# Mamba2 SSD and a low-rank mixer on one core: the sum of two operand parts is made on GpSimd in two operations instead of on VectorE in one

## The chip, the cores and the metric

The kernel runs on one core of one Trainium2 chip. The metric is the device time of one execution in microseconds (us); lower is better. The kernel before takes 227.7 us, the median of three runs (227.44 to 227.95).

A core has five engines that matter here: TensorE (PE; its weight loads are shown apart as PEld), VectorE (DVE), ScalarE (ACT), GpSimd (POOL) and the queue that issues transfers (SP). Each works off its own instructions in the order in which they were issued and waits on semaphores for the others.

## The reference

Two blocks follow each other. The first is a chunked state-space scan over 4 batches, 8 heads, 768 positions, head size 32 and state size 16. Its output, put back into (batch, position, 256 channels), is `x` of the second block:

```
def _moe_ref(x, U, V, w_ch1, w_ch2):
    xt = x.transpose(0, 2, 1)
    h = xt @ U @ V
    u = x + h.transpose(0, 2, 1)
    ch = np.maximum(u @ w_ch1, 0.0) @ w_ch2
    return (u + ch).astype(np.float32)
```

`w_ch1` is 256x1024 and `w_ch2` is 1024x256. The second block's weights arrive as 64-bit floats, which the kernel reads as pairs of 32-bit words and turns into float32; all else is float32.

## The kernel before

**Scan.** The scan goes over pairs of 128-position blocks. Its words in the plans are one-letter steps (`P`, `D`, `T`, `g`, `s`, `m`, `M`, `u`, `i`, `n`, `j`, `y`, `t`), each a short function that issues matmuls, VectorE masks and ScalarE copies.

**Mixer.** `mixer(b)` handles a batch in two halves (`j`) of 384 positions. `x` and `a` add the low-rank product to the scan's output; the result `u` lies as [128 channels, 2, 384]. Batch 0 multiplies in plain float32 (`plain`, word `U`). Batches 1 to 3 split each float32 factor into parts of a rounded format (`FP32R`) and sum three products:

- `near` is the factor times 1-2^-13, rounded; ScalarE makes it.
- `far` is the factor minus `near`; VectorE makes it.
- `both` is `far - near/4096` (`EPS` is 2^-12); `joined` makes it.

The weights have the matching three parts `w1[0..2]` and `w2[0..2]`, made once by `refine`. With `terms` the first two products (near with near, low with far) go into one PSUM bank, ScalarE scales the bank by 1+2^-12 (`scaled`), and the third product (the weights' `both` with the data's `both`) is added to it. So the third part is the last operand that TensorE reads in every sum.

**The steps.**

- `split(j)` (word `S`): near on ScalarE (L769), then `halves`: far on VectorE and `joined`, all three of 128x768, into one tile `u` that has one buffer. Batches 1 to 3 have two each, six in all.
- `first(j, m)` (word `f`): four matmuls into a bank `x` or `z`, two with near and two with far of `u`; then `scaled` (L779).
- `second(j, m)` (word `e`): two matmuls with `both` of `u`; then ScalarE makes near of the hidden activation (L808), with the ReLU.
- `third(j, m)` (word `h`): VectorE makes far of the activation from the bank and near (128x384). After every second `m`, a pair of 128x768 is whole, and `joined` makes its third part. Four pairs per half, 24 in all.
- `down(j)` or, for the second half of batch 3, `rows(j)` (word `d`): the products with `w2`, near first, far next, `both` last.

The parts of the hidden activation lie in a ring of 15 buffers called `words`, which the weights' words, two outputs and temporaries also use. Three buffers go to each pair.

**What sets the order.** The schedule is manual: `PLANS` lists the steps as words, and `follow` issues them one by one, so each engine's order is that of the words. Line 170 is the helper through which every VectorE operation passes, so all VectorE rows carry it; line 774 is `products`, through which the mixer's matmuls pass. GpSimd builds masks at the start (L294, L308, L309) and does four products and three slot products of the scan's first batch (L479, L591); the last of them starts at 20.84 us. All transfers are issued on SP.

A stretch of the plan of batch 4 (the last), with a split and what follows it:

```
'x1 h2.1.6 h2.1.7 d2.0 d2.1 a1.0 a1.1 d2.1 S1.0 d2.1 d2.1 d2.1 f1.0.0 d2.1 d2.1 f1.0.1 '
'd2.1 d2.1 e1.0.0 h1.0.0 e1.0.1 d2.1 d2.1 h1.0.1 f1.0.2 f1.0.3 d2.1 e1.0.2 f1.0.4 e1.0.3 '
...
'h1.0.6 h1.0.7 d1.0 d1.0 d1.0 d1.0 S1.1 d1.0 d1.0 f1.1.0 d1.0 f1.1.1 e1.1.0 d1.0 d1.0 '
```

Of the kernel before, what the change touches and what calls it, by code (L numbers as in the profile page):

```python
# [10 lines left out]
FP32 = mybir.dt.float32  # L11
# [10 lines left out]
EPS = 2.0 ** -12  # L22
AF = mybir.ActivationFunctionType
ALU = mybir.AluOpType
# [52 lines left out]
def kernel(  # L77
# [27 lines left out]
    nc = tc.nc  # L105
# [53 lines left out]
    class Kept:  # L159
# [15 lines left out]
    vector = Kept(nc.vector)  # L175
# [7 lines left out]
        out=a_sb,  # L183
# [128 lines left out]
    for v in range(2):  # L312
        half = slice(v * H, v * H + H)
        vector.tensor_tensor(out=ref[half, half], in0=upto[half, half],
                                in1=low[v][half, half], op=ALU.subtract)
# [13 lines left out]
    for g in range(2):  # L329
# [3 lines left out]
        out=la.rearrange("p b c h -> p b h c"),  # L333
        in0=la_ps.rearrange("p g (b h c) -> p (g b) h c", h=NH, c=NC),
        scalar1=1e-6, scalar2=1.0, op0=ALU.max, op1=ALU.min)
# [17 lines left out]
    for v in range(2):  # L353
        half = slice(v * H, v * H + H)
        vector.tensor_scalar(out=causal[half], in0=upto[half, half], scalar1=-1.0,
                                scalar2=None, op0=ALU.mult)
# [359 lines left out]
    def mixer(b):  # L716
# [37 lines left out]
        def halves(near, far, both, v):  # L754

            vector.tensor_tensor(out=far, in0=v, in1=near.bitcast(FP32), op=ALU.subtract)
            joined(near, far, both)

        def joined(near, far, both):

            vector.scalar_tensor_tensor(out=both, in0=near.bitcast(FP32), scalar=-EPS,
                                           in1=far.bitcast(FP32), op0=ALU.mult, op1=ALU.add)

        def split(j):

# [44 lines left out]
        def third(j, m):  # L810

            near, far, both = gs[j, m // 2]
            vector.scalar_tensor_tensor(
                out=far[:, m % 2], in0=gs["t", j, m], scalar=0.0,
                in1=near[:, m % 2].bitcast(FP32), op0=ALU.max, op1=ALU.subtract)
            if m % 2:
                joined(near, far, both)
# [210 lines left out]
```

## Time and profile before

| | |
|---|---|
| median of three runs | 227.7 us (227.44 to 227.95) |
| span of the profiled execution | 225.2 us |
| instructions | 6994 |
| granted TensorE clock | 1.00 |
| ScalarE waiting for TensorE's `x` bank, L779 | 27.6 us, 20 times |
| VectorE waiting for ScalarE's near, L808 | 16.6 us, 18 times |
| VectorE far of a pair's half, 128x384 | 48 operations, 0.55 us each |
| VectorE far of a split, 128x768 | 6 operations, 0.95 us each |
| transfers | 14.56 MB, 31.9% of the transfer engines' time |

The profile shows one execution. The span goes from the first to the last instruction; the 2.5 us between it and the median lie around the program. A row of a group names the line, the engine, the operation, the tiles (written <- read), the shape and the count; then busy time and the mean duration in ns, and after the second bar the time for which the engine stood idle before them, with what ended it. A row in order of time begins with start and duration in us. A row of waits gives the total in us, how often, and the longest.

### The profile page before, as it was taken

To read this page: it belongs to the slowest core of one execution; us is meant where nothing else is said; L and a number is where in the kernel's file an instruction comes from. 1 tells how busy PE (TensorE), PEld (TensorE's weight loads), DVE (VectorE), ACT (ScalarE), POOL (GpSimd) and SP (SyncE) were. 2 spreads that over 40 slices of the span, in tenths; PEclk is the share of its full clock that TensorE was granted. 3 is DMA by queue.
4 is the path that set the end of the run, shared out by engine and by line. 5 is a ranking of instruction groups with operands and counts; after the bars stand their busy time and mean duration, and the time that the engine had idled before them with its cause. 6 is when DMAs were issued, how large, how long until landed. Compare 5 with 4: busy or idle time off the path is not lost.

```text
span 225.2 us, 6994 instructions
## 1 busy us (share of the span) xinstructions
PE 217.0 (96%) x3016; PEld 180.5 (80%) x3016; DVE 157.3 (70%) x339; ACT 120.8 (54%) x283; POOL 6.2 (3%) x22
## 2 busy tenths in 40 slices
PE   7978899999999999999999999999999999999994
PEld 5657676665666678768999998799998799999993
DVE  3388899897996767879538827978557925765641
ACT  2353765579875425754616615385356434934820
POOL 4022000000000000000000000000000000000000
PEclk9999999999999999999999999999999999999999
DMA  6889779981950023642006200200000100010022
GB/s 89 141 120 147 113 171 220 240 177 41 167 76 4 0 73 41 89 59 73 4 3 90 75 1 3 76 0 0 4 0 3 43 30 0 3 68 3 0 70 70
DMA packets 69294, 14.56 MB, mean 65 GB/s; under 512 B 63568, under 2 KB 67472, under 8 KB 69264
## 3 DMA queue, kind: packets, MB, share of 16 engines
q1 hardware_dynamic: 69264, 14.13, 31.9%
q8 instruction: 23, 0.38, 0.7%
q14 instruction: 7, 0.06, 0.1%
HBM read 10.98 MB, written 3.15 MB: 63 GB/s over the span
## 4 chain that ended last, share of the span: by engine, by line
PE 89%; SPq 5%; DVE 2%; DMA 2%; issue 1%
PE x L774 33%; PE z L774 31%; SPq L196 4%; PE y L678 4%; PE y L654 4%; PE w L728 3%; PE w L901 2%; PE w L699 2%; PE x L528 2%; DMA bc<-in_C_dram 2%; PE w L496 2%; PE w L563 2%; PE x L739 2%; PE z L528 1%; PE z L739 1%
## 5 line engine op out<-in xcount | busy, mean ns | idle before, releaser
L170 DVE SCALAR_TENSOR_TENSOR words<-words 128x768 fp32r<-128x768 f32 (+6 forms) x44 | 34.6, 804 | 2.1 <-ACT words L420 1.1
L774 PE MATMUL z<-u,w 128*128 128x384 f32 x144 | 33.0, 349 | 0.0
L774 PE MATMUL x<-u,w 128*128 128x384 f32 x144 | 32.7, 346 | 0.0
L779 ACT ACTIVATE x<-x 128x384 f32<-128x384 f32 (+1 forms) x31 | 14.6, 470 | 28.2 <-PE x L774 27.6
L774 PEld LDWEIGHTS z<-u,w 128*128 128x128 f32 x144 | 25.0, 188 | 1.4 <-ACT z L779 0.2
L774 PEld LDWEIGHTS x<-u,w 128*128 128x128 f32 x144 | 24.9, 188 | 1.0
L774 PE MATMUL x<-words,w 128*128 128x384 f32 x120 | 24.7, 340 | 0.2 <-DVE yT L170 0.2
L774 PE MATMUL z<-words,w 128*128 128x384 f32 x120 | 24.6, 336 | 0.0
L779 ACT ACTIVATE z<-z 128x384 f32<-128x384 f32 (+1 forms) x30 | 14.2, 473 | 14.7 <-PE z L774 14.1
L170 DVE SCALAR_TENSOR_TENSOR words<-x,words 128x384 fp32r<-128x384 f32 x24 | 13.3, 553 | 11.7 <-ACT words L808 11.7
L774 PEld LDWEIGHTS x<-words,w 128*128 128x128 f32 x120 | 20.8, 188 | 0.5 <-DVE yT L170 0.4
L774 PEld LDWEIGHTS z<-words,w 128*128 128x128 f32 x120 | 21.1, 188 | 0.0
L170 DVE TENSOR_TENSOR yT<-x,yT 128x384 f32<-128x384 f32 x15 | 8.3, 553 | 16.0 <-PE x L774 15.4
L170 DVE SCALAR_TENSOR_TENSOR words<-z,words 128x384 fp32r<-128x384 f32 x24 | 13.2, 551 | 5.0 <-ACT words L808 5.0
L808 ACT ACTIVATE words<-x 128x384 fp32r<-128x384 f32 x24 | 11.8, 492 | 6.5 <-PE x L774 6.5
L808 ACT ACTIVATE words<-z 128x384 fp32r<-128x384 f32 x24 | 11.8, 492 | 4.5 <-PE z L774 4.5
L170 DVE TENSOR_TENSOR yT<-z,yT 128x384 f32<-128x384 f32 x15 | 8.3, 552 | 8.3 <-PE z L774 8.3
L654 PEld LDWEIGHTS y<-T,Sm 32*64 32x64 f32 x352 | 8.6, 131 | 4.7 <-issue 1.4
L654 PE MATMUL y<-T,Sm 32*64 32x64 f32 x352 | 11.9, 238 | 0.5 <-DVE settled L170 0.5
L678 PEld LDWEIGHTS y<-M,x 64*32 64x32 f32 x768 | 8.7, 105 | 4.5 <-issue 2.7
L678 PE MATMUL y<-M,x 64*32 64x64 f32 x768 | 11.3, 224 | 1.0 <-issue 0.7
L170 DVE SCALAR_TENSOR_TENSOR S<-S,kept,w 128x64 f32<-128x64 f32 x40 | 11.2, 279 | 1.6
(139 smaller groups left out, 382.3 us busy)
## 6 DMA issues: line engine op xcount, KB each, us to landing
words<-in_moe_w_ch_dram SPq DMA_DIRECT2D x7, 512.0 KB, 5.4
x<-in_x_dram SPq DMA_DIRECT2D x24, 128.0 KB, 3.5
out_dram<-o SPq DMA_DIRECT2D x5, 384.0 KB, 2.5
bc<-in_B_dram SPq DMA_DIRECT2D x24, 64.0 KB, 3.5
bc<-in_C_dram SPq DMA_DIRECT2D x12, 128.0 KB, 3.1
out_dram<-words SPq DMA_DIRECT2D x2, 384.0 KB, 3.6
words<-in_moe_w_ch_dram SPq DMA_DIRECT2D x2, 256.0 KB, 3.7
out_dram<-o SPq DMA_DIRECT2D x3, 128.0 KB, 1.7
```

Of the source, the lines that this page charges most:

```text
L170: self.last = call(*args, **kwargs)
L196: op = nc.sync.dma_start(**kwargs)
L496: nc.tensor.transpose(out=tp[:, i, v], in_=s["BC"][:, i, c + v].rearrange("p h n -> p (h n)"), identity=ident)
L528: nc.tensor.matmul(out=g[r][cols, c], lhsT=s["T"][rows, 0, c, cols], rhs=s["Cm"][rows, :, :, ts(2 * c + p, Q)].rearrange("r v t i -> r v i ...
L563: nc.tensor.matmul(out=s["A"][p][ts(r, Q), v], lhsT=s["bd"][half, v, 2 * r:2 * r + 2].rearrange("p h n -> p (h n)"), rhs=x_sb[k][half, v, ...
L654: product = nc.tensor.matmul(out=y[p][ts(r % 2, H), r // 2, c], lhsT=own[ts(r, Q)], rhs=s["T"][ts(r, Q), 1, :, ts(2 * c + p, Q)].rearrange ...
L678: product = nc.tensor.matmul(out=y[p][ts(i, Q), n, c], lhsT=x_sb[k][half, c, h], rhs=s["M"][half, h // 2, c, h % 2], start=fresh(k, p, [i] ...
L728: nc.tensor.matmul(out=p[ts(q, Q)], lhsT=U_sb[:, c], rhs=ytok[b][:, c, ts(q // 2, P)], start=(c == 0), stop=(c == NC - 1), skip_group_chec ...
L739: nc.tensor.matmul(out=h[q][:, :HS], lhsT=pT[rows], rhs=V4[rows], start=True, stop=True, skip_group_check=True)
L774: nc.tensor.matmul(out=t, lhsT=lhsT, rhs=rhs, start=start, stop=True, skip_group_check=True)
L779: nc.scalar.activation(t, t, AF.Copy, scale=1.0 + EPS)
L808: nc.scalar.activation(gs[j, m // 2][0][:, m % 2], t, AF.Relu, scale=NEAR)
```

## The change

`joined` no longer makes the third part in one VectorE operation. GpSimd first writes near times -2^-12 into the third part, and then adds far to it, in place. The value is the same, because the scaling by a power of two is exact. Both callers, `halves` (the splits) and `third` (the pairs), are affected; the weights' own third parts in `refine` stay on VectorE. No other line changes.

```diff
 def joined(near, far, both):
-    vector.scalar_tensor_tensor(out=both, in0=near.bitcast(FP32), scalar=-EPS,
-                                   in1=far.bitcast(FP32), op0=ALU.mult, op1=ALU.add)
+    nc.gpsimd.tensor_scalar(out=both, in0=near.bitcast(FP32), scalar1=-EPS, scalar2=None,
+                            op0=ALU.mult)
+    nc.gpsimd.tensor_tensor(out=both, in0=both.bitcast(FP32), in1=far.bitcast(FP32),
+                            op=ALU.add)
```

In the built programs VectorE has 30 operations fewer and GpSimd 60 more, in 30 pairs, after its last one of the prologue. The scaling waits for ScalarE (near) and for the buffer to be free; the addition waits for VectorE (far) and for the scaling. The order on TensorE, ScalarE and SP is the same. The scaling's line in the changed kernel is L761, the addition's L763.

## The prediction

> **What bounds the kernel now.** I read the busy shares first, then the chain that ended last, then a table of stages, and then TensorE's weight loads with their waits, since a busy matmul row alone proves little.
>
> ```profile
> PE 217.0 (96%) x3016; PEld 180.5 (80%) x3016; DVE 157.3 (70%) x339; ACT 120.8 (54%) x283; POOL 6.2 (3%) x22
> PE 89%; SPq 5%; DVE 2%; DMA 2%; issue 1%
> core 0: us, PE busy (x) PEld busy (x) DVE busy (x) ACT busy (x) POOL busy (x), PEclk, DMA share, GB/s
> 178.00:217.00 39.00, 38.86 (x240) 38.62 (x241) 23.36 (x36) 20.96 (x46) 0.00 (x0) 1.00 0.09 31
> ```
>
> The chain is TensorE for 89% and VectorE for 2%. In the stage from 178 to 217 us weight loads fill 38.62 of 39.00 us, at a granted clock of 1.00: there is nothing to win there. VectorE is busy for 60% of it. The changed line runs only after 80.8 us, and from 78 us on TensorE's weight loads wait for VectorE in six groups: 0.6, 0.4, 0.3, 0.2, 0.2 and 0.2 us, 1.9 us together. Three of them:
>
> ```profile
> PEld y L654 <- DVE settled L170: 0.6, 2, 0.4
> PEld x L774 <- DVE yT L170: 0.4, 1, 0.4
> PEld y L654 <- DVE S L170: 0.2, 1, 0.2
> ```
>
> **The change, part by part.** *Removed:* 30 VectorE operations (24 on `words`, 6 on `u`) of 0.958 us, 28.7 of its 157.3 us busy.
>
> ```profile
> L170 DVE SCALAR_TENSOR_TENSOR words<-words 128x768 fp32r<-128x768 f32 x24 | 23.0, 958 | 0.8
> L479 POOL TENSOR_TENSOR bd<-bc,FD 128x256 f32<-128x256 f32 x2 | 1.2, 620 | 7.4 <-ACT FD L385 7.4
> L479 POOL TENSOR_TENSOR bd<-bc,FD 128x128 f32<-128x128 f32 x2 | 0.8, 407 | 1.2 <-DMA bc<-in_B_dram 1.2
> L294 POOL TENSOR_SCALAR_AFFINE_SELECT low<-ones 128x128 f32<-128x128 f32 x2 | 0.5, 294 | 0.0
> L294 POOL TENSOR_SCALAR_AFFINE_SELECT after<-after 128x64 f32<-128x64 f32 x1 | 0.2, 240 | 0.1
> ```
>
> What this saves on the path is bounded above by the 1.9 us of waits. Most of it isn't there to be had: before the `yT` wait VectorE itself was idle, and the `settled` ones are a hand-over from TensorE and back. Only the 0.2 us for `S` (at 106.8 us) follows a removed operation. I take a gain of 0.1, between 0 and 0.2.
>
> *Added:* 60 GpSimd operations of 128x768. No row has them. The additions grow by (620-407)/128 = 1.66 ns an element, so 0.62+512x1.66 = 1.47 us; I use 1.45. The scaling has one input, like the selects: (294-240)/64 = 0.84 ns an element, 0.294+640x0.84 = 0.83 us. With 0.07 us between two dependent GpSimd operations (the gap in the prologue's selects) one sum takes 2.35 us, 30 take 70 us, half of the 137 us from 80 to 217. From below, DVE's 0.96 us for one pass bounds each; from above I allow twice my price (4.7 us a sum), as the formats with rounded output never ran on GpSimd here.
>
> The Trainium skill speaks against the change. "GPSIMD Engine Reference", § 3.1 Elementwise, gives a two-input addition of 2048 elements 4497 ns on GpSimd; at that rate 768 take 1.69 us, an estimate, and site F below would lose 0.7 us more over its three additions.
>
> *Moved:* the scaling waits for near alone, which ScalarE ends about 1 us before VectorE has made far, so on a free GpSimd it hides beside far, and the sum comes 1.45-0.96 = 0.5 us later than before. GpSimd's queue holds nothing else after 20.84 us: no DMA is issued there, none is passed. Behind a waiting addition stands the next scaling, nothing more. ScalarE's and VectorE's writes into the rings now wait for GpSimd's reads of the same buffer, but that buffer is some five pairs old; I cost this at nothing, hidden by that distance.
>
> *Who needs the sum, and when.* It is the last operand of its product. For the 24 pairs the products with near and with far come first, 32 matmuls that start 0.12 to 0.17 us apart, a cover of about 4 us; the last pair, far done at 215.2, gets its sum at about 217.1, and the products that use it start near 218.0. For the six splits the first readers are the two matmuls of `second`. Far's end plus 1.5 us against that reader: 83.3 against 86.2 (A); 106.0 against 106.2 (B); 147.1 against 147.3 (C); 161.5 against 163.2 (D, behind a pair); 182.0 against 185.7 (E). The sixth (F) comes behind two pairs:
>
> ```profile
> 195.94 0.96 DVE L170 SCALAR_TENSOR_TENSOR words<-words 128x768 fp32r<-128x768 f32 x1
> 197.86 0.96 DVE L170 SCALAR_TENSOR_TENSOR words<-words 128x768 fp32r<-128x768 f32 x1
> 198.74 0.95 DVE L170 TENSOR_TENSOR u<-yT,u 128x768 fp32r<-128x768 f32 x1
> 199.72 0.96 DVE L170 SCALAR_TENSOR_TENSOR u<-u 128x768 fp32r<-128x768 f32 x1
> 201.86 0.51 PE L774 MATMUL x<-u,w 128*128 128x384 f32 x2
> ```
>
> Far of the first pair is ready at 195.90, so GpSimd runs addition, scaling, addition, scaling, addition from 196.2: 3x1.45+2x0.83+4x0.07 = 6.3, to 202.5. The matmul wanted it at 201.8: TensorE stalls 0.7 us, and being full it never makes that up.
>
> *The unknown: both engines reading SBUF at once.* At a split, GpSimd's scaling and VectorE's far wait for the same near. Far has two SBUF operands. At C there is no room:
>
> ```profile
> 143.65 0.84 ACT L769 ACTIVATE u<-yT 128x768 fp32r<-128x768 f32 x1 [0.95 <-DVE yT L170]
> 144.62 0.95 DVE L170 TENSOR_TENSOR u<-yT,u 128x768 fp32r<-128x768 f32 x1
> 145.62 0.30 PEld L774 LDWEIGHTS x<-u,w 128*128 128x128 f32 x2
> ```
>
> Near ends at 144.49, far at 145.57, and the weight load that goes with far's first product starts 0.05 us later. If far had to wait out a scaling begun at 144.49, it would end 0.7 us later, and so would TensorE. The lower bound is no hindrance. The nearest rows:
>
> ```profile
> 10.70 1.20 POOL L479 TENSOR_TENSOR bd<-bc,FD 128x256 f32<-128x256 f32 x2 [7.37 <-ACT FD L385]
> 11.78 0.41 DVE L170 TENSOR_TENSOR BC<-bc,F 128x256 f32<-128x256 f32 x1
> ```
>
> They overlap for 0.12 us, and VectorE's 0.41 us are its usual ones. That is too short to tell. The upper bound is waiting in full: A 0.15, B 0.4 (far behind the scaling, 0.33, the rest behind `bd`), C 0.7, D 0.3 (0 to 0.55, by who goes first), E 0, and F 1.3 in place of 0.7 (1.0 if the far of the split waits for a pair's addition, 1.6 if it goes before a scaling); 2.85 in all.
>
> "SBUF — State Buffer", § Who interferes with whom, says that a VectorE instruction with two SBUF inputs and a GpSimd one that reads SBUF lock each other out in full. By that rule the sum is its upper bound, +2.75; without it, +0.6.
>
> **The sum.** No hindrance: 0.7-0.1 = +0.6. Full waiting: 2.85-0.1 = +2.75. The overlap row can't choose, so I take the middle, +1.7. The profiled execution spans 225.2 us, the runs' median is 227.7: 2.5 us around the span that nothing here touches. 225.2+1.7+2.5 = **229.4 us**.
>
> **The rivals.**
>
> *Latency alone* (+0.6, 228.3 us): only F stalls. For it: the overlap row shows no lengthening. Against it: that overlap is 0.12 us.
>
> *GpSimd becomes the bound.* At 4.7 us a sum the 30 need 141 us from 80.8 on, to 221.8; from the first product of the last sum to the end are 7.2 us (218.0 to 225.2): 229.0+2.5 = 231.5. In the last stage, where ten sums come in the 34.7 us from 180.5 to 215.2, stalls that can't be made up would bring it near 235. It decides from 3.5 us a sum. For it: unseen operations. Against: rows that make 2.35.
>
> *VectorE was the hidden limit* (faster). In front of the 0.2 to 0.6 us waits stands VectorE's in-order queue with 0.96 us sums in it; freed of them it brings S, M, yT and ytok earlier. At most 1.9 us: 225.8. It decides if a waiting TensorE had a removed sum directly ahead on VectorE, and GpSimd's reads cost VectorE under 0.2 us. Against: weight loads at 99% in the last stage, VectorE idle before `yT`.
>
> *It does nothing* (227.7): the sums hide, F included, if GpSimd's additions take under 1.2 us.
>
> **Chances.** A measurement here tells about 0.2% (0.46 us) from no change. Latency with waiting in part or full 0.55, latency alone 0.22 (0.12 of it within 0.2%), GpSimd as bound 0.12, relief 0.08, nothing 0.03. So faster 0.08, same 0.15, slower 0.77. The range leaves out half of the GpSimd bound and most of relief: its low end is just under no change (227.5), its top lies above full waiting (227.7+2.75 = 230.5) and one us into the bound's 231.5 to 235, at 232.5.
>
> **What would show it.** Right: GpSimd rows at L761 and L763 of 0.8 and 1.45 us, 60 of them, some 70 us; VectorE at 129 us unless lengthened; a new TensorE wait for GpSimd at F of 0.7 us or more; far of the splits late by up to 0.8 us, C the clearest. Wrong: a scaling far above 0.83 us, a sum late in the pairs' products, or VectorE's one-SBUF-input rows (0.55 us) longer beside GpSimd, which would delay everything and isn't in my sum. Unmoved rows and no new wait mean that nothing happened.

## The result, and the profile after

The changed kernel takes 259.92 us (median of four runs, 258.03 to 260.15) against 227.82 us (227.44 to 228.01) for the kernel before, measured together: a ratio of 1.138, 95% interval 1.135 to 1.142, or 32.1 us more. The forecast was 229.4 us with a range up to 232.5. Its direction held; its size was off by a factor of about 19 (+1.7 expected, +32.1 found).

The profiled execution spans 257.9 us, 32.7 more than before. First its page: busy time by engine, the granted clock in 40 slices, the chain that ended last, and the new groups.

```profile
PE 228.9 (89%) x3016; PEld 189.9 (74%) x3016; DVE 133.3 (52%) x309; ACT 121.7 (47%) x283; POOL 127.5 (49%) x82
...
PEclk9999999999999999979999997997799999959989
...
PE 59%; POOL 21%; issue 7%; SPq 5%; DVE 4%; ACT 2%; DMA 1%; POOLq 1%; ACTq 0%; DVEq 0%
...
L761 POOL TENSOR_SCALAR words<-words 128x768 fp32r<-128x768 f32 x24 | 51.3, 2137 | 30.8 <-ACT words L810 29.6
L763 POOL TENSOR_TENSOR words<-words 128x768 fp32r<-128x768 f32 x24 | 44.2, 1843 | 2.0
L761 POOL TENSOR_SCALAR u<-u 128x768 fp32r<-128x768 f32 x6 | 15.0, 2495 | 72.6 <-ACT u L771 72.2
```

The scaling takes 2.14 us where 0.83 was forecast, the addition 1.84 where 1.45 was. With two gaps of about 0.08 us a sum holds GpSimd for 4.1 us, not 2.35. GpSimd stands for 21% of the chain, TensorE for 59% instead of 89%. GpSimd's mean share of 49% hides that it has no free time in long stretches, of which the longest are 89.4 to 110.7, 157.7 to 178.2, 187.5 to 204.1 and 210.65 to 227.1 us.

Next TensorE's weight loads after 78 us, by what they waited for (total us, times, longest):

```profile
PEld x L776 <- POOL u L763: 15.2, 5, 7.0
PEld x L776 <- POOL words L763: 5.9, 3, 3.4
PEld x L776 <- DVE u L170: 1.6, 1, 1.6
```

That is 22.7 us of new waits. The span splits another way without remainder: TensorE was busy for 217.0 us before and idle for 225.2-217.0 = 8.2; after it was busy for 228.9 and idle for 29.0. So 20.8 us are idle time and 11.9 us are the same 3016 matmuls taking longer. The granted clock accounts for most of the latter: its mean is 0.954, not 1.00, and TensorE's busy time multiplied by the missing share of the clock, summed over windows of one microsecond, gives 10.6 us.

The longest stall shows both. GpSimd in order of time, ahead of the last split (site F of the prediction):

```profile
210.65 2.13 POOL L761 TENSOR_SCALAR words<-words 128x768 fp32r<-128x768 f32 x1 [0.81 <-ACT words L810]
212.87 1.85 POOL L763 TENSOR_TENSOR words<-words 128x768 fp32r<-128x768 f32 x1
214.80 2.14 POOL L761 TENSOR_SCALAR words<-words 128x768 fp32r<-128x768 f32 x1
217.02 1.85 POOL L763 TENSOR_TENSOR words<-words 128x768 fp32r<-128x768 f32 x1
218.96 2.13 POOL L761 TENSOR_SCALAR words<-words 128x768 fp32r<-128x768 f32 x1
221.17 1.80 POOL L763 TENSOR_TENSOR words<-words 128x768 fp32r<-128x768 f32 x1
223.05 2.13 POOL L761 TENSOR_SCALAR u<-u 128x768 fp32r<-128x768 f32 x1
225.27 1.80 POOL L763 TENSOR_TENSOR u<-u 128x768 fp32r<-128x768 f32 x1
```

And ScalarE's near for the last of these pairs and for the split, then TensorE, all of the same execution:

```profile
214.31 0.52 ACT L810 ACTIVATE words<-z 128x384 fp32r<-128x384 f32 x1
214.70 0.87 ACT L771 ACTIVATE u<-yT 128x768 fp32r<-128x768 f32 x1
...
219.54 0.86 PE L776 MATMUL z<-u,w 128*128 128x384 f32 x4
227.12 1.01 PE L776 MATMUL x<-u,w 128*128 128x384 f32 x2 [6.72 <-POOL u L763]
227.93 1.48 PE L776 MATMUL z<-words,w 128*128 128x384 f32 x4
```

The split's near is there at 215.57, but its scaling starts at 223.05: 7.5 us behind the pairs in GpSimd's queue. TensorE has done what stands ahead of the split's sum by 220.4 and stands still. The four matmuls before the stall take 0.86 us, the four after it 1.48 us. The same place in windows of one microsecond (length; busy us and count of PE, PEld, DVE, ACT and POOL; granted clock; transfers):

```profile
224.00:225.00 1.00, 0.00 (x0) 0.00 (x0) 0.00 (x0) 0.00 (x0) 1.00 (x1) 1.00 0.00 0
225.00:226.00 1.00, 0.00 (x0) 0.00 (x0) 0.00 (x0) 0.00 (x0) 0.92 (x2) 0.61 0.00 0
226.00:227.00 1.00, 0.00 (x0) 0.00 (x0) 0.00 (x0) 0.00 (x0) 1.00 (x1) 0.50 0.00 0
...
231.00:232.00 1.00, 1.00 (x5) 1.00 (x4) 0.00 (x0) 0.49 (x1) 0.06 (x1) 0.50 0.00 0
232.00:233.00 1.00, 1.00 (x7) 1.00 (x7) 0.55 (x2) 0.00 (x0) 1.00 (x1) 0.97 0.00 0
```

Here the clock falls to half about 5 us after the last matmul and is back about 5 us after the next one. That is not its rule: at C a standstill of 1.87 us was enough, and the clock fell at about 157.0, when TensorE was already at work again (two rows of TensorE, then a window):

```profile
153.36 0.85 PE L776 MATMUL x<-u,w 128*128 128x384 f32 x4
156.08 0.62 PE L776 MATMUL x<-u,w 128*128 128x384 f32 x2 [1.86 <-POOL u L763]
...
156.00:160.00 4.00, 3.92 (x14) 3.93 (x15) 1.20 (x3) 2.27 (x6) 2.25 (x3) 0.62 0.00 0
```

In windows of 0.2 us this execution has five stretches at half clock: three of 3.4 us and two of 6.8 us. "TensorE: Matmul & The Clock Gate", Part 1, in the Trainium skill states a half rate after an idle window of about 3.4 us and full rate after a busy one as long. The trace agrees on the two rates (0.50 and 1.00) and, by the length of the low stretches, on the window; that a shorter standstill can be enough is what it shows beyond this.

Last, the two engines at SBUF, at the split B:

```profile
104.19 1.83 POOL L763 TENSOR_TENSOR words<-words 128x768 fp32r<-128x768 f32 x1
104.33 2.51 DVE L170 TENSOR_TENSOR u<-yT,u 128x768 fp32r<-128x768 f32 x1
```

VectorE's far takes 2.51 us instead of 0.95: it begins 0.14 us after GpSimd's addition and ends 0.82 us after it. At C it is the other way about: far (from 151.20) and the scaling (from 151.18) start within 0.02 us of each other, far keeps its 0.95 us, and the scaling takes 2.96 us instead of 2.13.

### The profile page after: what moved, and what is told of

It reads as the page before. It is cut to its first block, busy times and chain, and to the rows that moved or that the text cites. A ratio compares the mean times of both kernels' runs of the same rounds, so it can differ in the third digit from the quotient of the medians.

```text
span 257.9 us, 7092 instructions
## 1 busy us (share of the span) xinstructions
PE 228.9 (89%) x3016; PEld 189.9 (74%) x3016; DVE 133.3 (52%) x309; ACT 121.7 (47%) x283; POOL 127.5 (49%) x82
## 4 chain that ended last, share of the span: by engine, by line
PE 59%; POOL 21%; issue 7%; SPq 5%; DVE 4%; ACT 2%; DMA 1%; POOLq 1%; ACTq 0%; DVEq 0%
PE x L776 22%; PE z L776 21%; POOL words L761 8%; POOL words L763 6%; SPq L196 4%; POOL u L763 4%; POOL u L761 3%; PE y L678 3%; PE y L654 3%; PE w L728 2%; DVE words L170 2%; PE x L528 1%; PE w L699 1%; DMA bc<-in_B_dram 1%; PE w L496 1%
## 5 line engine op out<-in xcount | busy, mean ns | idle before, releaser
L761 POOL TENSOR_SCALAR words<-words 128x768 fp32r<-128x768 f32 x24 | 51.3, 2137 | 30.8 <-ACT words L810 29.6
L761 POOL TENSOR_SCALAR u<-u 128x768 fp32r<-128x768 f32 x6 | 15.0, 2495 | 72.6 <-ACT u L771 72.2
L776 PE MATMUL x<-u,w 128*128 128x384 f32 x144 | 36.3, 372 | 14.9 <-POOL u L763 13.6
L763 POOL TENSOR_TENSOR words<-words 128x768 fp32r<-128x768 f32 x24 | 44.2, 1843 | 2.0
L776 PEld LDWEIGHTS x<-u,w 128*128 128x128 f32 x144 | 27.2, 206 | 17.6 <-POOL u L763 15.2
L776 PE MATMUL z<-u,w 128*128 128x384 f32 x144 | 34.9, 365 | 0.0
L776 PE MATMUL x<-words,w 128*128 128x384 f32 x120 | 26.9, 358 | 2.0 <-POOL words L763 1.8
L776 PEld LDWEIGHTS z<-u,w 128*128 128x128 f32 x144 | 26.8, 200 | 1.4 <-ACT z L781 0.2
L776 PE MATMUL z<-words,w 128*128 128x384 f32 x120 | 26.8, 358 | 0.0
L776 PEld LDWEIGHTS z<-words,w 128*128 128x128 f32 x120 | 23.0, 203 | 0.0
L654 PE MATMUL y<-T,Sm 32*64 32x64 f32 x352 | 11.9, 238 | 0.6 <-DVE settled L170 0.6
```

The costliest lines, as they stand in the source:

```text
L654: product = nc.tensor.matmul(out=y[p][ts(r % 2, H), r // 2, c], lhsT=own[ts(r, Q)], rhs=s["T"][ts(r, Q), 1, :, ts(2 * c + p, Q)].rearrange ...
L761: nc.gpsimd.tensor_scalar(out=both, in0=near.bitcast(FP32), scalar1=-EPS, scalar2=None, op0=ALU.mult)
L763: nc.gpsimd.tensor_tensor(out=both, in0=both.bitcast(FP32), in1=far.bitcast(FP32), op=ALU.add)
L776: nc.tensor.matmul(out=t, lhsT=lhsT, rhs=rhs, start=start, stop=True, skip_group_check=True)
```

## The experiments

Two theories had to be told apart. The first, the queue (Q where a letter is used): a sum costs GpSimd 4.1 us by itself, so sums pile up. The second, the ports (P): GpSimd's reads and VectorE's two-operand operations keep each other waiting, so both are slow and everything behind them too. All ratios are against the kernel before in the same series.

### Only the six splits, and only the 24 pairs

```diff
-        def joined(near, far, both):
+        def joined(near, far, both, pool=True):
+            if pool:
                 nc.gpsimd.tensor_scalar(...)
                 nc.gpsimd.tensor_tensor(...)
+            else:
+                vector.scalar_tensor_tensor(...)
...
             if m % 2:
-                joined(near, far, both)
+                joined(near, far, both, False)
```

This is the first, with the calls shortened. The second passes `False` in `halves` and leaves the pairs' call as it was.

> The six sums of the splits are made on GpSimd as in the change, the 24 sums of the pairs on VectorE as before. Theory Q (queue: a sum takes GpSimd 2.13+1.84 us, and TensorE waits for sums that stand in GpSimd's queue behind others): without pairs ahead of them the splits wait only for their own 4 us. Site A, D and E hide it, B loses about 1.7, C about 2.2, F about 0.4: 4.3 us, so 232 us (230 to 234), granted clock above 0.98. Theory P (port: GpSimd's reads of SBUF lengthen VectorE's work, and that costs the time): a fifth of the GpSimd work, a fifth of the 32 us, 234 us.

> The 24 sums of the pairs are made on GpSimd, the six of the splits on VectorE. Theory Q: the last pair's sum ends near 221 where 218.0 is wanted, 3 us, with a lower clock after it 1.5 more, and one or two us at the other halves: 234 us (231 to 238). With the splits alone this comes to far less than the 32 us of both, as the long stalls (7.0, 3.1 us) arise where a split stands behind three pairs. Theory P: four fifths of the GpSimd work, four fifths of the loss, above 250 us.

The splits alone take 231.47 us against 227.28 (ratio 1.019, 1.013 to 1.024), inside the range of the queue theory and 2.5 us under the 234 of the ports. The pairs alone take 242.62 us (1.066, 1.060 to 1.072), between the two expectations: a miss for both. The rows of TensorE's waits for GpSimd, the splits alone first:

```profile
PEld x L780 <- POOL u L764: 2.9, 2, 2.2
```

```profile
PEld x L780 <- POOL words L764: 9.0, 5, 3.8
```

The parts add up to 4.2+15.3 = 19.5 us, while both together cost 32. The other 12.6 us appear only when both share one queue: then a split waits behind its pairs, as at F. Part of this difference is the clock after the longer stalls: busy time multiplied by the missing clock is 3.4 us in the profiled execution of the pairs alone and nothing in that of the splits alone, against 10.6 us with both. (These two executions were the fastest of their kernels, so the difference at the medians is smaller.)

### VectorE makes every sum, GpSimd does the same work into memory that nothing reads

```diff
+    spare = const.tile([P, 2, 384], FP32, name="spare")
...
+            vector.scalar_tensor_tensor(out=both, in0=near.bitcast(FP32), scalar=-EPS,
+                                           in1=far.bitcast(FP32), op0=ALU.mult, op1=ALU.add)
-            nc.gpsimd.tensor_scalar(out=both, in0=near.bitcast(FP32), scalar1=-EPS, scalar2=None,
+            nc.gpsimd.tensor_scalar(out=spare, in0=near.bitcast(FP32), scalar1=-EPS, scalar2=None,
                                     op0=ALU.mult)
-            nc.gpsimd.tensor_tensor(out=both, in0=both.bitcast(FP32), in1=far.bitcast(FP32),
+            nc.gpsimd.tensor_tensor(out=spare, in0=spare, in1=far.bitcast(FP32),
                                     op=ALU.add)
```

To make room, a constant of ones moved into another tile's memory, here and in the two spare kernels below.

> VectorE makes all sums as before; GpSimd also does the change's two operations for each of the 30, into a spare buffer that nobody reads. (The constant of ones lies in another buffer for the room.) GpSimd's load is that of the change, and no engine waits for its results. Theory Q: TensorE has no wait for GpSimd; only VectorE's operations with two SBUF operands lengthen (far of the splits, the sums): 228 to 234 us, clock 0.99 or more. Theory P: the same time as the change, 250 us or more.

It takes 240.53 us (1.059, 1.055 to 1.063), a miss for both expectations. That number misleads: no weight load of the mixer waits for GpSimd, and VectorE's last operation is this, with that of the kernel before (from its chain) behind it:

```profile
229.72 0.42 DVE L170 TENSOR_TENSOR o<-x,words 128x256 f32<-128x256 f32 x1 [0.52 <-PE x L779]
```

```profile
222.01 0.42 DVE o L170
```

The output is made by 230.1 of a span of 238.7 us; the rest is GpSimd working off what had piled up, two sums of 4.1 us each. A consumer of these sums would have had to wait for them, which is argued here and not shown. The output itself is 7.7 us later than in the kernel before (230.1 against 222.4), though TensorE waits for no result of GpSimd's there: VectorE's sums for the pairs, with two operands in SBUF, took 1.22 us instead of 0.96. So the run shows a cost of the ports beside a queue that piles up, and doesn't part the two.

### The operations by themselves

The kernel before, with eight GpSimd operations behind its last VectorE operation, into memory that nothing reads; the diff shows four of them.

```diff
+    late(nc.gpsimd.tensor_scalar(out=t0, in0=A, scalar1=-EPS, scalar2=None, op0=ALU.mult))
...
+    nc.gpsimd.tensor_copy(out=t2, in_=A)
+    nc.gpsimd.tensor_tensor(out=t1, in0=A, in1=A2, op=ALU.add)
...
+    nc.gpsimd.tensor_scalar(out=r0, in0=A, scalar1=-EPS, scalar2=None, op0=ALU.mult)
```

> The kernel before, and after its last VectorE operation eight GpSimd operations on finished data, with VectorE idle: scaling of 768 and of 384 elements, a copy of 768, an addition of 768 and of 256, a product of 256 with a broadcast operand as in the scan, and scaling and addition of 768 with the rounded output format. Only their durations count, not the time. If the price is the operation's own: scaling 2.13 us and addition 1.84 us in both formats. If it is the rounded format: 0.83 and 1.45 us in the plain one. If it is VectorE's company: 0.83 and 1.45 us in both.

A single execution, of which only the durations count (the whole took 237.21 us). GpSimd in order of time, with VectorE idle:

```profile
223.38 2.13 POOL L1009 TENSOR_SCALAR plainout<-yT 128x768 f32<-128x768 f32 x1 [201.77 <-DVE o L170]
225.58 1.17 POOL L1010 TENSOR_SCALAR plainout<-yT 128x384 f32<-128x384 f32 x1
226.81 0.82 POOL L1011 COPY plainout<-yT 128x768 f32<-128x768 f32 x1
227.60 1.80 POOL L1012 TENSOR_TENSOR plainout<-yT 128x768 f32<-128x768 f32 x1
229.36 0.72 POOL L1013 TENSOR_TENSOR plainout<-yT 128x256 f32<-128x256 f32 x1
230.04 0.61 POOL L1014 TENSOR_TENSOR plainout<-yT,slot 128x256 f32<-128x256 f32 x1
230.74 2.13 POOL L1020 TENSOR_SCALAR roundout<-yT 128x768 fp32r<-128x768 f32 x1
232.93 1.80 POOL L1021 TENSOR_TENSOR roundout<-yT 128x768 fp32r<-128x768 f32 x1
```

The scaling takes 2.13 us alone, as in the changed kernel, so neither VectorE nor the rounded output makes it dear. By the two lengths it costs (2.13-1.17)/384 = 2.5 ns an element. The copy, also with one input, takes 0.82 us: nearly the 0.83 forecast for the scaling. And a product with a broadcast operand, the kind of row from which the addition was priced, is cheaper than a plain addition of the same size (0.61 against 0.72); whether the product or the broadcast makes it so isn't shown.

"GPSIMD Engine Reference", § 4.1 Engine selection, in the Trainium skill calls GpSimd about 2x slower for two inputs and "roughly line-rate" for one. The copy's 0.82 us fits this, beside the 0.96 us of VectorE's removed sum; the scaling's 2.13 us, also with one input, does not.

### The scaling on ScalarE

```diff
-            nc.gpsimd.tensor_scalar(out=both, in0=near.bitcast(FP32), scalar1=-EPS, scalar2=None,
-                                    op0=ALU.mult)
+            nc.scalar.activation(both, near.bitcast(FP32), AF.Copy, scale=-EPS)
```

> ScalarE makes the scaling (near times -1/4096, 128x768), GpSimd only the addition. A sum takes GpSimd 1.84+0.08 us, under the 3.5 us from which ten sums fit into the last stage. Theory Q: the queue is gone, splits lose under 1 us each, ScalarE's 30 added operations of about 0.85 us cost 1 to 2: 228.5 to 233 us, clock 0.98 or more. Theory P: half of the GpSimd work, half of the loss, 244 us.

236.43 us (1.040, 1.035 to 1.045), a miss between the two. GpSimd now has 1.9 us a sum, and weight loads wait for it for 2.2 us in all; they also wait for ScalarE, 2.3 us for `words` and 1.0 for its scaling of `x`. Whether ScalarE's 30 more operations of 0.85 us were the price needed the next kernel.

### The addition alone

The same kernel without the scaling: GpSimd adds the unscaled near to far. The scaling is left out of the computation; nothing takes its place.

```diff
-            nc.gpsimd.tensor_scalar(out=both, in0=near.bitcast(FP32), scalar1=-EPS, scalar2=None,
-                                    op0=ALU.mult)
-            nc.gpsimd.tensor_tensor(out=both, in0=both.bitcast(FP32), in1=far.bitcast(FP32),
+            nc.gpsimd.tensor_tensor(out=both, in0=near.bitcast(FP32), in1=far.bitcast(FP32),
                                     op=ALU.add)
```

> The change without its scaling: GpSimd adds near and far, unscaled, for all 30 sums (the third operand has another value, so the output differs; it leaves out the scaling). Beside scale_on_act (236.4 us) it tells what ScalarE's 30 added operations cost. A sum takes GpSimd 1.80 us. If ScalarE was the price there: 229 to 232 us. If it was the waiting between VectorE and GpSimd: 234 to 237 us.

229.67 us against 227.93 (1.008, 1.005 to 1.012), as expected. So ScalarE's operations cost the last kernel 236.4-229.7 = 6.7 us (7.4 when each is set against its own kernel before), and the whole change costs 1.7 us when a sum takes GpSimd 1.9 us. This is the row left of TensorE's waits for GpSimd:

```profile
PEld x L774 <- POOL u L761: 1.2, 3, 0.6
```

### A copy in the scaling's place

The scaling by -1/4096 is left out; near is copied instead. GpSimd still issues two dependent operations for each sum, but the first is a cheap one.

```diff
-            nc.gpsimd.tensor_scalar(out=both, in0=near.bitcast(FP32), scalar1=-EPS, scalar2=None,
-                                    op0=ALU.mult)
+            nc.gpsimd.tensor_copy(out=both, in_=near.bitcast(FP32))
```

> The change, with the scaling replaced by a GpSimd copy of near (the third operand has another value, so the output differs; it leaves out the scaling by -1/4096). The number of operations, their waits and the data read stay; only the first operation's price falls, from 2.13 to 0.82 us, and a sum's from 4.1 to 2.8. If the loss is the scaling's price, that carries GpSimd past 3.5 us a sum: 230 to 234 us, clock 0.99 or more, waits of TensorE for GpSimd under 4 us. If it is the second operation and its hand-over, or the reads, whatever they cost: above 245 us.

234.53 us against 227.96 (1.029, 1.025 to 1.033), half a microsecond above the range expected, with the clock (0.993) and TensorE's waits for GpSimd (3.8 us in all) as expected. From its groups, and then from its waits:

```profile
L762 POOL TENSOR_TENSOR words<-words 128x768 fp32r<-128x768 f32 x24 | 44.8, 1867 | 4.0 <-DVE words L170 2.4
...
L761 POOL CAST words<-words 128x768 fp32r<-128x768 f32 x24 | 21.9, 914 | 37.1 <-ACT words L809 37.1
```

```profile
PEld x L775 <- POOL u L762: 3.5, 4, 2.5
```

Two dependent operations, the same operands and the same order, with 1.2 us less for the first: +6.6 us instead of +32.1. So some 25 us of the loss hang on the scaling's price alone. In the order of GpSimd's time for a sum the losses are 1.7 us (1.9), 6.6 us (2.9 with the gaps) and 32.1 us (4.1): a bend between the last two, as of a queue that fills up, though a longer scaling also reads SBUF for longer; what that costs comes with the ports below.

### TensorE kept busy in the stalls

The changed kernel, with matmuls into an unread bank ahead of the first `second` of four splits: enough to fill about 2 us at B, C and D and about 6 us at F.

```diff
             t = gs["t", j, m]
+            if m == 0:
+                n = {(1, 1): 8, (2, 0): 8, (2, 1): 8, (3, 1): 28}.get((b, j), 0)
+                if n:
+                    idle(bank("w", 4 * P), n)
             products(t, terms(j, m, (2,)), False)
```

> The change, with spare matmuls into a free bank put ahead of the first products with a split's sum at the four sites that stall over 2 us: two of 512 columns at three sites, seven at the last split. They wait for nothing that GpSimd does. If TensorE's standstill lowers the clock, and the low clock is a part of the loss of its own: granted clock 0.97 to 0.98 in place of 0.954, and 253 to 257 us. If the clock falls for another reason: no change, or slower by what the spare matmuls take.

254.02 us (1.117, 1.112 to 1.122), 5.9 us less than the changed kernel (5.5 when each is set against its own kernel before), at a mean clock of 0.985 instead of 0.954. TensorE at F in this kernel, the fillers first:

```profile
218.21 6.17 PE L140 MATMUL w<-ident 128*128 128x512 f32 x14
225.10 0.62 PE L776 MATMUL x<-u,w 128*128 128x384 f32 x2 [0.72 <-POOL u L763]
225.55 0.86 PE L776 MATMUL z<-words,w 128*128 128x384 f32 x4
```

The four matmuls behind the wait take 0.86 us again. More work made the kernel faster: part of the loss is the clock, which falls after TensorE has stood still, and some of that comes back when the stalls are filled. GpSimd takes no less time for a sum.

### The ports alone: reading against writing

Two kernels in which VectorE makes all sums as before, and GpSimd does idle work at the same 30 places. In the first it adds near and far into unread memory; in the second it only writes, three memsets of 0.74 us after far is made.

```diff
+            nc.gpsimd.tensor_tensor(out=spare, in0=near.bitcast(FP32), in1=far.bitcast(FP32),
+                                    op=ALU.add)
```

```diff
+            for n in range(3):
+                op = nc.gpsimd.memset(spare, 0.0)
```

> VectorE makes all sums as before; GpSimd adds near and far into a spare buffer that nobody reads, 30 operations of 1.84 us that each read two operands from SBUF. No queue forms and nobody waits for GpSimd. If reading at once makes VectorE's two-operand operations wait: the far of the splits and VectorE's sums lengthen, 229 to 232 us. If it costs nothing: 227.5 us.

> As spare_add, but GpSimd fills the spare buffer three times with zeros (about 0.74 us each) at each of the 30 places, after far is made: as long a load on GpSimd, writing, but reading nothing. If the reads are what VectorE waits for: 227.5 us, VectorE's rows as before. If any GpSimd load slows the kernel: as spare_add.

The reading kernel takes 237.36 us against 227.38 (1.043, 1.038 to 1.048), dearer than either expectation, and no tail of GpSimd's is in it: its last addition ends at 230.0, VectorE's last operation at 233.9. The writing one takes 228.20 (1.002, 0.9995 to 1.005), where no change was expected if only reads matter. First the addition that reads, with what VectorE does then, in order of time, and behind it the group of `bd`:

```profile
93.64 0.96 DVE L170 SCALAR_TENSOR_TENSOR words<-words 128x768 fp32r<-128x768 f32 x1
93.75 2.52 POOL L764 TENSOR_TENSOR spare<-words 128x768 f32<-128x768 f32 x1 [0.38 <-DVE words L170]
94.51 2.03 DVE L170 TENSOR_TENSOR bd<-bc,FD 128x256 f32<-128x256 f32 x1
```

```profile
L170 DVE TENSOR_TENSOR bd<-bc,FD 128x256 f32<-128x256 f32 x9 | 8.6, 961 | 0.0
```

The same group beside the memsets:

```profile
L766 POOL MEMSET spare<- 128x768 f32 x90 | 66.6, 740 | 129.6 <-DVE u L170 79.2 <-DVE words L170 46.4
...
L170 DVE TENSOR_TENSOR bd<-bc,FD 128x256 f32<-128x256 f32 x9 | 3.7, 417 | 0.0
```

VectorE's sum starts at 93.64; GpSimd's addition, 0.11 us later, takes 2.52 us instead of 1.80. VectorE's next product, with two operands in SBUF, waits for the rest of it: 2.03 us instead of 0.42. Each waits for the one that began first. Beside memsets `bd` keeps its 417 ns. "SBUF — State Buffer", § Who interferes with whom, in the Trainium skill says this: a VectorE instruction with two SBUF inputs and a GpSimd one that reads lock each other out, and one that only writes does not. The ports theory is right as a mechanism. As the main cause of the 32 us it is not: with the same reads by the addition, but the sums off VectorE, the kernel of the addition alone loses 1.7 us. The busy times of the changed kernel speak against it as well. VectorE is busy for 133.3 us, where 157.3-28.7 = 128.6 were left without the sums, so 4.7 us longer in all; GpSimd's 60 operations take 121.3 us, where their prices alone (30 times 2.13+1.80) make 117.9, so 3.4 us longer. TensorE waited for VectorE's far once, 1.6 us, against 21.1 us for GpSimd.

### Only sums that nobody waits for

GpSimd makes the first two pairs of each half, 12 sums; VectorE the rest.

```diff
             if m % 2:
-                joined(near, far, both)
+                joined(near, far, both, m < 4)
```

(`halves` passes `False`; `joined` has the argument `pool` as above.)

> Only the first two pairs of each half (12 sums) are made on GpSimd; the last two pairs and the splits stay on VectorE. These 12 sums are needed latest of all: after the other pairs and 32 matmuls. If the loss comes from GpSimd's queue, TensorE never waits for GpSimd here, and what is left are VectorE's operations that wait for its reads: 227.5 to 230 us. If every sum on GpSimd costs the same share of what pairs_only lost (15 us for 24): 235 us.

228.80 us against 227.93 (1.004, 1.000 to 1.007), with no weight load of the mixer waiting for GpSimd. The operations are as dear as before, but they come with time to spare. There is no gain either: taking 12 sums off VectorE gave nothing. No kernel of this series was faster than the one before.

## Why the prediction was wrong

**The step that failed is the scaling's price.** "The scaling has one input, like the selects ... 0.83 us." It is 2.13 us. The prediction had itself named "a scaling far above 0.83 us" as a sign of being wrong, and its price lay below its own lower bound of 0.96 us for one operation. The selects' slope is close to the price of a copy (0.82), and that a scaling costs what a copy costs was an assumption without a row. The addition was mis-sized too, 1.45 against 1.80 to 1.84, from rows of products with a broadcast operand, which run cheaper here. The sum "2.35 us" is 4.1, within the upper bound of 4.7 that the prediction stated. Being over its 3.5 us threshold, it changes the case, not only the size.

**"GpSimd becomes the bound"** was a rival with a chance of 0.12, and it is what happened. Its threshold fits the runs on both sides of it: 2.9 us a sum cost 6.6 us, 4.1 us a sum 32.1. Its time, "231.5 to 235", does not. It took the throughput of 30 sums and the tail behind the last, as though GpSimd could start each sum when it liked and TensorE had other work meanwhile. Left out were the order in the queue (the split at F, near done at 215.57, is scaled at 223.05, and TensorE waits 7.0 us for it), that several stalls of this sort add up on a full TensorE (20.8 us more idle time), and the clock after them (10.6 of 11.9 us more busy time).

**F alone, by 0.7 us**: F stalled for 7.0 us, and the weight loads waited for GpSimd at seven more places. The pairs were counted as covered by "about 4 us"; they waited three times, 3.4 us the longest. The waits of writers for GpSimd's reads of a buffer, put at nothing, came to one of 1.5 us on VectorE.

**Waiting at SBUF.** Its mechanism was right and was named: far of a split late, by who goes first. At B it cost 1.6 us on TensorE, where the upper bound had 0.4, since far met a pair's addition that ran late. Where VectorE keeps its sums, a case that the prediction did not price, it cost 10.0 us (the kernel of spare additions); the bound of 2.85 counted the splits' fars and, at B, `bd`, but no other two-operand rows.

**VectorE's relief** was put at 0.1 us. No run shows a gain over the kernel before from fewer sums on VectorE, though the relief is worth something against the waiting at SBUF: additions on GpSimd cost 1.7 us when VectorE is rid of its sums and 10.0 us when it isn't.

**What held**: the order in GpSimd's queue, the count of 60 rows, and a small loss for a change that loads GpSimd lightly. That the addition alone took 229.67, close to 229.4, is partly luck: it has 1.9 us a sum, not 2.35. A straight line between its +1.7 us and the +6.6 us of 2.9 us a sum puts 2.35 at about +3.9, an estimate, so even at its own price the forecast would have been some 2 us low.

**What stays open.** How the 32.1 us divide between waits and clock isn't settled to the microsecond: the trace counts 20.8 of idle and 11.9 of slowed time, and filling four stalls brought back 5.9. What length of standstill brings the clock down isn't shown either: in the kernel of spare additions it fell after one of 1.81 us at 208.1 and not after one of 1.70 us at 165.6. The size of the loss with the pairs alone (15.3 us) was not explained in advance by any theory, though its largest row is a 9.0 us wait for GpSimd.

## What to carry to other kernels

Price an operation on another engine from a row of the same operation, not from one with the same number of inputs; where there is none, put a few copies of it behind the last instruction of a kernel and read the durations, before trusting any sum. An engine that has 50% of its time to spare on average can still be the bound: lay its work in the order of its queue against the time between two deadlines in the tightest stage, and ask what urgent operation stands behind a less urgent one. A stall on TensorE can cost more than its own length, since the clock may fall after it.

## What the runs showed of the hardware

- On GpSimd a multiplication by a constant (2.13 us for 128x768) is dearer than an addition of two operands of that size (1.80 us), and 2.6 times a copy (0.82 us). Output in the rounded format costs nothing more.
- The granted TensorE clock was 1.00 or 0.50, and 0.50 for 3.4 or 6.8 us at a time, after standstills of 1.87 to 6.7 us in the changed kernel; matmuls of 128x384 then go 0.32 us apart instead of 0.174 us. Spare matmuls in the stalls saved 5.9 us.
- GpSimd's reads and VectorE's operations with two SBUF operands shut each other out (an addition 2.52 us instead of 1.80 behind a VectorE sum; `bd` 961 ns instead of 417 on average); writes by GpSimd leave it at 417 ns.
